# Low parts on VectorE instead of GpSimd behind attention, and weight conversions spread over w_out's products

## The chip, the cores and the metric

The kernel runs on one core of a Trainium2 chip. That core has a matrix engine (TensorE, PE in the profile, with its weight loads as PEld), three engines for elementwise work (VectorE, called DVE; ScalarE, called ACT; GpSimd, called POOL) and SyncE (SP), which here only issues DMAs. The metric is the device time of one execution in microseconds; lower is better. The kernel before took 1270.37 us, the median of three runs (1267.63 to 1270.51).

## What is computed

The reference is block-causal attention followed by a bilinear feed-forward layer, all in float32:

```python
# q, k, v: (8, 8, 576, 64), blocks of 64
scores = scale * np.matmul(q, k.transpose(0, 1, 3, 2))
scores = np.where(block_i >= block_j, scores, -1000000000.0)
attn = softmax(scores)                      # with 1e-09 in the denominator
x = (attn @ v) as (4608, 512)               # tokens x model width
a = x @ w_a ; b = x @ w_b                   # 512 -> 1536
out = (a * b) @ w_out                       # 1536 -> 512
```

The weights w_a, w_b and w_out come as float64 and are turned into float32 parts on the chip. h stands for a * b below.

## The kernel before, in words

**Number format.** TensorE multiplies in a faster float32 format of less precision. To keep precision, each operand is split into a high part (a rounding copy, made by ScalarE) and a low part (the value less its high part, a subtraction on VectorE or GpSimd). A product is then three products: high by high, high by low, low by high. `split` (L108) makes both parts: L110 is ScalarE's copy, L113 the subtraction, on the engine it is handed as `lo_eng`.

**Stages.** The hidden width of 1536 is worked in twelve blocks of 128, called f. First comes attention, head by head, and woven into it the *first pass* (`first_pass`, L545) for the blocks f = 0 to 3: for 288 tokens at a time, `ab_unit` (L228) makes a and b by 24 products each pair, multiplies them (hf, L243) and splits the result (hh by ScalarE, hl by `lo_eng[0]`, which is GpSimd, L245); `o_unit` multiplies with w_out. What of the first pass is left when the attention loop ends (L638) is emitted behind it (L784 and L796), together with the conversion of the weights for the blocks 4 to 7.

Then comes the *second pass*, for the blocks 4 to 11. It runs twice over six tiles of 768 tokens: once for the blocks 4 to 7 (tiles 0 to 5 in the text) and once for 8 to 11 (tiles 6 to 11). A tile has four units (`pair_unit`, L701), one for each f, and then w_out's products (`pair_out`, L743). A unit makes a and b for two halves of 384 tokens at once, with seven products of sums in place of eight: `sums_x` (L669) makes sums and differences of parts of x, splits them into seven high parts (L680 to L684, ScalarE) and seven low parts (L689 to L692), and that for two halves kp = 0 and 1 of the model width. A unit has 42 matmuls of 384 columns in the order y, x, w, v and then the second parts of x, w, v, each of six (twelve in a tile's first unit are taken in another order). Between them VectorE does seven operations, L729 to L739: u = x + y at L729, for which the second part of x's product waits, t = w + u at L731, for which w's waits, and so on, up to the two halves of h at L736 and L739. ScalarE makes h's high parts, GpSimd its low parts (L737 and L740). `pair_out` is 96 matmuls, run without a break in the program's order.

**Low parts of x's sums.** For kp = 0 all four instructions are on VectorE; for kp = 1 the first two (L689, L690) are on VectorE, the last two (L691, L692) on GpSimd.

**Weight conversions.** `convert_w` (L180) is a generator: each step emits a few instructions. A part of w_a and w_b (8 for four blocks) takes six steps, a part of w_out (4) five: on VectorE L139, L143, L145, L147, L149 one by one (the fifth with four small ones at L172 for the sums), ScalarE's at L140, L165 and L175, and at the end the low parts (L177, L178, or L113 for w_out). A part's raw data are fetched ahead on SyncE's queue. The parts for the blocks 8 to 11 are made during tiles 1 to 5, laid into a staging buffer `st` and stored to DRAM by SyncE's queue; they are loaded again in tile 5.

**What sets the order.** A planner at compile time orders each engine's instructions: by their place in the program and by when its model says that they can start. On the chip each engine then runs its list in order. `background(now)` (L777) fixes where in the program a conversion step stands: one step for each STEP or STEP2 ns of products counted in `k` at 2.4 columns per ns. In the second pass `k` counts the units' products (L834), not w_out's. `behind_of(ins, key)` (L117) tells the planner to put an instruction behind the last one noted under that key: conversions behind the last "hf" (L739 of the unit before), x's low parts behind "hf", and those on GpSimd behind "la" (h's last low part).

Of the kernel before, what the change touches and what calls it, by code (L numbers as in the profile page):

```python
# [14 lines left out]
ALU = mybir.AluOpType  # L15
# [23 lines left out]
MORE = 6  # L39
PREF = True  # L40
STEP = 800
STEP2 = 1900
LATE = 1
LO2 = lambda nc: nc.vector
CONVP = [1]*12
# [7 lines left out]
def attention_then_bilinear_ffn(  # L53
# [10 lines left out]
    nc = tc.nc  # L64
# [13 lines left out]
    T2 = 384  # L78
# [26 lines left out]
    def f32(ap):  # L105
        return ap.bitcast(F32)
# [10 lines left out]
    def behind_of(ins, key):  # L117
        if key in last:
            tc.add_manual_dep(ins.ins, last[key].ins.name, NOSYNC, reason="after work that is waited for")
# [35 lines left out]
    def parts(fs):  # L155
        return [(f, i) for f in fs for i in range(KP)] + [(f, KP) for f in fs]

    def new_wo(f):
        w_sb[f][1] = wopool.tile([P, 2, DO], F32R, tag="wo", name=f"wo{f}")
# [49 lines left out]
    lo_eng = [nc.gpsimd]  # L209
# [427 lines left out]
                n_moe += 1  # L637
    order.close()  # L638
    marks.clear()
    right.close()  # L640
    ps_more = ctx.enter_context(
        tc.tile_pool(name="ps_more", bufs=MORE, space=bass.MemoryType.PSUM, reuse_waits="tile"))
# [3 lines left out]
    def bank(nm):  # L646
        nonlocal n_bank
        n_bank += 1
        return (ps_mm if n_bank % 8 < 2 else ps_more).tile([P, 512], F32, tag="mm", name=nm)
# [7 lines left out]
    def new_w(f):  # L657
        w_sb[f] = [w2.tile([P, KP, 2, NW, P], F32R, tag="wab", name=f"wab{f}"), None]

    def load_x(tt):  # L660

        raw = []
        for cc in range(NCC):
            raw.append(rpool.tile([P, 2, T2], F32, tag="xr", name=f"xr{cc}_{tt}"))
            nc.sync.dma_start(
                raw[cc].rearrange("p j n -> p (j n)"), xd[cc * P:(cc + 1) * P, 2 * tt * T2:2 * (tt + 1) * T2])
        return raw

    def sums_x(raw, kp, nm):  # L669

        hi = xk.tile([P, NW, T2], F32R, tag="xh", name=f"xh_{nm}_{kp}", bufs=3)
        t = tpool.tile([P, 3, T2], F32, tag="xt", name=f"xt_{nm}_{kp}")
        a, b = raw[2 * kp:2 * kp + 2]
        v = nc.vector
        for ins in (v.tensor_tensor(t[:, 1], b[:, 1], a[:, 1], op=ALU.subtract),
                    v.tensor_tensor(a[:, 1], a[:, 1], a[:, 0], op=ALU.subtract)):
            if nm == f"0_{NT2}":
                behind_of(ins, "hf")
        v.tensor_tensor(t[:, 0], b[:, 1], a[:, 1], op=ALU.subtract)
        nc.scalar.copy(hi[:, 0:2], a)  # L680
        nc.scalar.copy(hi[:, 2:4], t[:, :2])
        v.tensor_tensor(t[:, 2], b[:, 0], t[:, 0], op=ALU.subtract)
        nc.scalar.copy(hi[:, 4:6], b)
        nc.scalar.copy(hi[:, 6], t[:, 2])  # L684
        yield
        lo = xk.tile([P, NW, T2], F32R, tag="xl", name=f"xl_{nm}_{kp}", bufs=2)
        e = nc.gpsimd if kp else v
        for k, ins in enumerate((
                v.tensor_tensor(lo[:, 0:2], a, f32(hi[:, 0:2]), op=ALU.subtract),  # L689
                v.tensor_tensor(lo[:, 2:4], t[:, :2], f32(hi[:, 2:4]), op=ALU.subtract),  # L690
                e.tensor_tensor(lo[:, 4:6], b, f32(hi[:, 4:6]), op=ALU.subtract),  # L691
                e.tensor_tensor(lo[:, 6], t[:, 2], f32(hi[:, 6]), op=ALU.subtract))):  # L692
            if nm[0] == "0" and nm != "0_0":
                behind_of(ins, "la" if k > 1 and kp else "hf")
        yield hi, lo


# [45 lines left out]
    def pair_out(fs, hs, nm, out):  # L743

        todo = [(j, o) for j in (1, 0) for o in range(NO)]
        n = {}

        def run(j, o, fs_):
            k = j, o
            if k not in n:  # L750
                n[k] = 0, bank(f"pso{j}_{o}_{nm}")[:, :T2]
            i, ps = n[k]
            osl = slice(o * P, (o + 1) * P)
            for f in fs_:
                (hh, hl), wt = hs[f][j], w_sb[f][1]
                for a, b in ((0, hh), (0, hl), (1, hh)):
                    nc.tensor.matmul(ps, wt[:, a, osl], b, start=i == 0, stop=i == 3 * len(fs) - 1)  # L757
                    i += 1
            n[k] = i, ps
            if i == 3 * len(fs):  # L760
                out(j, o, ps)

        for k in todo[:2]:
            run(*k, fs[:-1])
        for k in todo[:2]:
            run(*k, fs[-1:])
        for k in todo[2:]:
            run(*k, fs)

    for f in range(F1, F1 + F2):  # L770
        new_w(f)
# [5 lines left out]
    def background(now):  # L777
        nonlocal n_conv
        while n_conv < now:
            next(conv, None)  # L780
            n_conv += 1

    k = 0
# [8 lines left out]
    for kp in range(KP):  # L792
        g = sums_x(raw, kp, "0_0")
        next(g)
        xs.append(next(g))
# [3 lines left out]
    start, pace = k * HT / 2.4 / STEP, STEP  # L799
    k = 0  # L800


    for ps_ in range(2):
        fs = list(range(F1 + ps_ * F2, F1 + (ps_ + 1) * F2))
        for tt in range(NT2):
            lastp = ps_ == 1 and tt == NT2 - 1
            pt = {}

            def load_part(j, o):
                ts = slice((2 * tt + j) * T2, (2 * tt + j + 1) * T2)  # L810
                pt[j, o] = ppool.tile([P, T2], F32, tag="pt", name=f"pt{j}_{o}_{tt}_{ps_}"), ts
                if ps_ == 1:
                    nc.sync.dma_start(pt[j, o][0], part[o * P:(o + 1) * P, ts])

            def out(j, o, ps):
                t, ts = pt[j, o]
                if ps_ == 0:
                    nc.scalar.copy(t, ps)
                    nc.gpsimd.dma_start(part[o * P:(o + 1) * P, ts], t, accum_op=ALU.add)
                else:  # L820
                    nc.vector.tensor_tensor(t, ps, t, op=ALU.add)
                    nc.sync.dma_start(outT[o * P:(o + 1) * P, ts], t)
                i = todo.index((j, o)) + 6
                if i < len(todo):
                    load_part(*todo[i])

            todo = [(j, o) for j in (1, 0) for o in range(NO)]
            hs = {}
            nm = f"z{ps_}_{tt}"
            for i, f in enumerate(fs):  # L830
                if ps_ == 0 and tt == 0:
                    background(PER_F * (i + 1))
                for _ in pair_unit(f, xs, f"{nm}_{f}", hs, i == 0):
                    k += 1  # L834
                    background(start + k * T2 / 2.4 / pace)
                if i == 0 and not lastp:
                    raw = load_x((tt + 1) % NT2)
                if i == 1:
                    for x in todo[:6]:
                        load_part(*x)  # L840
                if i == 2 and not lastp:
                    nxt = [sums_x(raw, kp, f"{ps_}_{tt + 1}") for kp in range(KP)]
                    next(nxt[0])
                if ps_ == 0 and tt == NT2 - 1:
                    new_w(f + F2)
                    for kp in range(KP):
                        nc.sync.dma_start(
                            f32(w_sb[f + F2][0][:, kp]).rearrange("p j c n -> p (j c n)"), wabd[f - F1, kp])
            if not lastp:
                lo0 = next(nxt[0])  # L850
                next(nxt[1])
                xs = [lo0, next(nxt[1])]
            if ps_ == 0 and tt == 0:
                background(1e4)
                conv = convert_w(parts(range(F1 + F2, NF)), nc.vector, paced=True, stage=stage)
                n_conv, start, k, pace = 0, 0, 0, STEP2
            pair_out(fs, hs, nm, out)
            if ps_ == 0 and tt == NT2 - 1:
                background(1e4)
                for f in fs:  # L860
                    new_wo(f + F2)
                    nc.sync.dma_start(f32(w_sb[f + F2][1]).rearrange("p j n -> p (j n)"), wod[f - F1])
# [39 lines left out]
```

## Time and profile before

| what | value |
|---|---|
| median of three runs | 1270.37 us |
| the profiled execution | 1273.42 us, its span 1271.7 us |
| granted TensorE clock, mean | 0.994 |
| busy: PE / VectorE / ScalarE / GpSimd | 97% / 78% / 55% / 47% |
| attention's end, about | 640 us |
| w_out's products of tile 0, the part that waits last | from 733.40 us |
| a tile of the second run (1019.05 to 1065.52) | 46.47 us |

The profile shows one execution. A row of a timeline has start, length, engine, line and operation, outputs and inputs, and in brackets how long the engine stood idle before it and what ended that. A row of a group has line, engine, operation, names and shape, count, then busy time and mean ns, then the idle time before. The chain of waits is the work that ended last, followed backwards. Names: xl and xh are the low and high parts of x's sums, hl and hh (or h_z in the second pass) those of h, hf is h before the split, u_z the seven operations' results, psx_z and its like a unit's products, pso and pso_z w_out's, raww, sw, mw, xw and st the stages of a conversion, pt and part the partial output.

### The profile page before, as it was taken

Reading aid. Unit: us, or ns where it says so; the run is one execution under the profiler, and the core shown is the slowest. Engines: PE = TensorE matmul, PEld = TensorE weight load, DVE = VectorE, ACT = ScalarE, POOL = GpSimd, SP = SyncE. Lnnn points to the kernel's source line nnn. Section 1 sums busy time; section 2 is a strip of 40 time slices with the busy share of each in tenths; the row PEclk is TensorE's granted clock in tenths of the full one; section 3 lists DMA queues with packets and bytes.
Section 4 is the critical chain, followed back from the end, with each engine's and each line's share of the span. In section 5 each row is a group of like instructions: output and inputs, shape, how many; then the busy total and the mean of one; then the engine's idle time right before and its main releaser. Section 6 shows DMA issues by size and latency. Waiting matters only on the chain.

```text
span 1271.7 us, 23478 instructions
## 1 busy us (share of the span) xinstructions
PE 1238.1 (97%) x7849; PEld 1171.8 (92%) x7849; DVE 986.7 (78%) x2341; ACT 701.6 (55%) x1770; POOL 596.7 (47%) x727
## 2 busy tenths in 40 slices
PE   9998999999999999999998999999999999999998
PEld 5667998999999999999997999999999999999998
DVE  6888887877877877878789989889869577577553
ACT  4788887788788788877745434244334222122210
POOL 3667666565665665655522254254354323123231
PEclk9899999999999999999998999999999999999999
DMA  5467667767667776677224364464477542243131
GB/s 179 124 179 205 171 173 198 180 167 183 163 177 181 177 179 171 166 180 170 88 92 120 104 142 132 123 146 136 118 173 275 154 149 83 67 149 102 49 100 63
DMA packets 86585, 187.15 MB, mean 147 GB/s; under 512 B 11200, under 2 KB 46016, under 8 KB 86464
## 3 DMA queue, kind: packets, MB, share of 16 engines
q1 hardware_dynamic: 74944, 166.76, 47.0%
q0 software_dynamic: 6912, 9.44, 5.1%
q10 hardware_dynamic: 4608, 9.44, 2.0%
q8 instruction: 63, 1.03, 0.3%
q14 instruction: 58, 0.48, 0.1%
HBM read 87.03 MB, written 47.19 MB: 106 GB/s over the span
## 4 chain that ended last, share of the span: by engine, by line
PE 75%; DVE 15%; issue 3%; ACT 3%; DMA 2%; POOL 1%; SPq 0%; ACTq 0%; DVEq 0%; POOLq 0%
PE pso_z L757 16%; PE ps L217 12%; PE tp L468 7%; PE psw_z L711 6%; PE psx_z L711 6%; PE psv_z L711 5%; PE pso L217 5%; PE s L392 4%; PE av L517 3%; PE av L523 3%; PE psy_z L711 3%; PE sl L392 2%; DVE sw L147 2%; DVE nm L398 1%; DMA kp<-kT 1%
## 5 line engine op out<-in xcount | busy, mean ns | idle before, releaser
L113 POOL TENSOR_TENSOR h_z<-u_z,h_z 128x384 fp32r<-128x384 f32 x96 | 110.2, 1149 | 331.7 <-ACT h_z L110 315.1
L217 PE MATMUL ps<-xh,wab 128*128 128x288 f32 x1024 | 241.6, 303 | 1.2 <-ACT a L241 1.2
L445 POOL TENSOR_SCALAR e<-e,rc 128x512 f32<-128x512 f32 (+3 forms) x256 | 151.1, 602 | 130.5 <-DVE rc L442 122.6
L757 PE MATMUL pso_z<-h_z,wo 128*128 128x384 f32 x1152 | 203.0, 335 | 0.7 <-POOL h_z L113 0.7
L757 PEld LDWEIGHTS pso_z<-h_z,wo 128*128 128x128 f32 x1152 | 199.8, 188 | 1.9 <-POOL h_z L113 1.9
L217 PEld LDWEIGHTS ps<-xh,wab 128*128 128x128 f32 x1024 | 171.9, 188 | 4.7 <-ACT a L241 1.4
L472 DVE TENSOR_TENSOR al<-tp,ah 128x512 fp32r<-128x512 f32 x224 | 131.5, 608 | 30.3 <-ACT ah L470 29.8
L217 PE MATMUL ps<-xl,wab 128*128 128x288 f32 x512 | 154.0, 301 | 0.0
L470 ACT CAST ah<-tp 128x512 fp32r<-128x512 f32 x224 | 116.5, 532 | 51.6 <-PE tp L468 48.8
L468 PE MATMUL tp<-ident,e 128*128 128x128 f32 x832 | 134.7, 276 | 8.2 <-POOL e L445 3.0
L110 ACT CAST h_z<-u_z 128x384 fp32r<-128x384 f32 x96 | 49.3, 514 | 161.5 <-DVE u_z L736 157.4
L217 PE MATMUL pso<-hh,wo 128*128 128x288 f32 x512 | 128.4, 312 | 4.4 <-ACT hh L110 4.4
L711 PE MATMUL psx_z<-xh,wab 128*128 128x384 f32 x384 | 117.8, 342 | 5.6 <-DVE u_z L729 5.2
L401 ACT ACTIVATE e<-s,nm 128x192 f32<-128x192 f32 (+2 forms) x192 | 101.4, 528 | 36.1 <-DVE nm L398 26.9
L468 PEld LDWEIGHTS tp<-ident,e 128*128 128x128 f32 x832 | 100.0, 140 | 22.4 <-issue 9.5
L711 PE MATMUL psw_z<-xh,wab 128*128 128x384 f32 x384 | 116.9, 340 | 0.5 <-DVE u_z L731 0.4
L711 PE MATMUL psv_z<-xh,wab 128*128 128x384 f32 x384 | 116.5, 338 | 0.1
L398 DVE TENSOR_REDUCE nm<-s 128x1 f32<-128x192 f32 (+3 forms) x256 | 109.9, 431 | 2.4
L217 PEld LDWEIGHTS ps<-xl,wab 128*128 128x128 f32 x512 | 96.4, 188 | 3.4
L217 PEld LDWEIGHTS pso<-hh,wo 128*128 128x128 f32 x512 | 88.7, 192 | 6.6 <-ACT hh L110 5.3
L113 POOL TENSOR_TENSOR v<-vr,v 128x320 fp32r<-128x320 f32 x56 | 50.2, 896 | 87.5 <-ACT v L110 72.7
L392 PE MATMUL s<-k,q 128*128 128x256 f32 x336 | 81.0, 321 | 2.5 <-ACT e_s L401 2.1
(144 smaller groups left out, 2970.4 us busy)
## 6 DMA issues: line engine op xcount, KB each, us to landing
k<-kp SPq DMA_DIRECT2D x112, 288.0 KB, 3.7
xr<-xd SPq DMA_DIRECT2D x48, 384.0 KB, 3.5
q<-qp SPq DMA_DIRECT2D x112, 160.0 KB, 2.6
raww<-wab SPq DMA_DIRECT2D x24, 512.0 KB, 3.7
qp<-qT SPq DMA_DIRECT2D x32, 320.0 KB, 3.2
vr<-vm SPq DMA_DIRECT2D x64, 160.0 KB, 2.9
kp<-kT SPq DMA_DIRECT2D x32, 288.0 KB, 3.3
xd<-xf ACTq DMA_DIRECT2D x32, 288.0 KB, 3.1
```

The costliest lines, as they stand in the source:

```text
L110: nc.scalar.copy(hi, src)
L113: return lo_eng.tensor_tensor(lo, src, f32(hi), op=ALU.subtract)
L217: mm = nc.tensor.matmul(ps, w_, d_, start=(i == 0), stop=(i == n - 1))
L392: mark = nc.tensor.matmul(ps[:, :w], qm[:, q0[t]:q0[t] + P], kk[:, :w], start=(i == 0), stop=(i == len(ks) - 1))
L398: nc.vector.tensor_reduce(nm[:, t:t + 1], view, axis=AX.X, op=ALU.max, negate=True)
L401: nc.scalar.activation(out, view, AF.Exp, bias=bias, accum_out=sm[:, t, :1])
L445: nc.gpsimd.tensor_scalar(ev, ev, rc[:, t:t + 1], 1.0, op0=ALU.mult, op1=ALU.mult)
L468: mark = nc.tensor.transpose(tp[:, c], src, ident)
L470: nc.scalar.copy(ah[:, :m, cols], tp[:, :m])
L472: return nc.vector.tensor_tensor(al[:, :m, cols], tp[:, :m], f32(ah[:, :m, cols]), op=ALU.subtract)
L711: nc.tensor.matmul(ps, wt[:, i, iw], j[:, ix], start=start and kp == 0 and i == 0 and j is xh, stop=kp == KP - 1 and i == 1, skip_group_ch ...
L757: nc.tensor.matmul(ps, wt[:, a, osl], b, start=i == 0, stop=i == 3 * len(fs) - 1)
```

## The change

Three edits. The low parts of h of the first pass that are emitted behind the attention loop go to VectorE. All low parts of x's sums go to VectorE, all ordered behind "hf". And `pair_out` becomes a generator: after each of w_out's products the caller counts it in `k` and may emit conversion steps, while the pace STEP2 goes from 1900 to 3200 ns for a step.

```diff
-STEP2 = 1900
+STEP2 = 3200
...
     order.close()
     marks.clear()
+    lo_eng[0] = nc.vector
...
         lo = xk.tile([P, NW, T2], F32R, tag="xl", name=f"xl_{nm}_{kp}", bufs=2)
-        e = nc.gpsimd if kp else v
-        for k, ins in enumerate((
+        for ins in (
                 v.tensor_tensor(lo[:, 0:2], a, f32(hi[:, 0:2]), op=ALU.subtract),
                 v.tensor_tensor(lo[:, 2:4], t[:, :2], f32(hi[:, 2:4]), op=ALU.subtract),
-                e.tensor_tensor(lo[:, 4:6], b, f32(hi[:, 4:6]), op=ALU.subtract),
-                e.tensor_tensor(lo[:, 6], t[:, 2], f32(hi[:, 6]), op=ALU.subtract))):
+                v.tensor_tensor(lo[:, 4:6], b, f32(hi[:, 4:6]), op=ALU.subtract),
+                v.tensor_tensor(lo[:, 6], t[:, 2], f32(hi[:, 6]), op=ALU.subtract)):
             if nm[0] == "0" and nm != "0_0":
-                behind_of(ins, "la" if k > 1 and kp else "hf")
+                behind_of(ins, "hf")
...
                 for a, b in ((0, hh), (0, hl), (1, hh)):
                     nc.tensor.matmul(ps, wt[:, a, osl], b, start=i == 0, stop=i == 3 * len(fs) - 1)
                     i += 1
+                    yield
...
         for k in todo[:2]:
-            run(*k, fs[:-1])
+            yield from run(*k, fs[:-1])
         for k in todo[:2]:
-            run(*k, fs[-1:])
+            yield from run(*k, fs[-1:])
         for k in todo[2:]:
-            run(*k, fs)
+            yield from run(*k, fs)
...
-            pair_out(fs, hs, nm, out)
+            for _ in pair_out(fs, hs, nm, out):
+                k += 1
+                background(start + k * T2 / 2.4 / pace)
```

## The prediction

> **What bounds the kernel now.** I read the page's busy shares first, then the table of stretches from the end of attention on, then the chain of waits, and last single instructions in order of time.
>
> ```profile
> PE 1238.1 (97%) x7849; PEld 1171.8 (92%) x7849; DVE 986.7 (78%) x2341; ACT 701.6 (55%) x1770; POOL 596.7 (47%) x727
> ```
>
> TensorE (PE) is nearly always busy, so only its holes can be won. The change touches nothing ahead of attention's end, so the holes that count lie from about 640 us on, in two places.
>
> ```profile
> 640.00:660.00 20.00, 19.11 (x143) 18.66 (x142) 19.80 (x39) 7.75 (x19) 5.27 (x5) 1.00 0.30 99
> 660.00:680.00 20.00, 17.65 (x131) 17.21 (x131) 19.38 (x43) 9.33 (x22) 4.10 (x4) 1.00 0.34 109
> 680.00:700.00 20.00, 16.11 (x96) 15.09 (x94) 19.52 (x33) 12.46 (x25) 7.10 (x5) 0.83 0.47 138
> 700.00:716.50 16.50, 16.50 (x94) 16.26 (x94) 16.50 (x32) 7.76 (x13) 2.37 (x3) 1.00 0.46 156
> 716.50:733.40 16.90, 16.16 (x89) 15.05 (x88) 16.55 (x31) 8.38 (x15) 6.24 (x6) 1.00 0.09 31
> ```
>
> **Place A, 640 to 733 us** (columns: stretch, length, PE, weight load, VectorE, ScalarE, GpSimd, granted clock, DMA share, GB/s): the rest of the first pass and the units of the second pass's first tile, under the conversion of the next weights. VectorE is busy 91.75 of 93.40 us, 98%; PE stands for 7.87 us, and from 680 to 700 us its clock is 0.83. So here VectorE sets the pace.
>
> ```profile
> 747.02 0.53 PE psy_z L711 x3
> ...
> 972.73 16.64 PE pso_z L757 x96
> ...
> 1019.05 16.79 PE pso_z L757 x96
> ...
> 1065.52 16.78 PE pso_z L757 x96
> ```
>
> **Place B, tiles 1 to 5 of the second pass** (chain of waits: start, length, what). Tile 0's products end about 747.02, tile 5's at 972.73 + 16.64 = 989.37: five tiles in 242.35 us, 48.47 each. From 1019.05 to 1065.52, where nothing is converted any more, a tile takes 46.47. So the five lose 242.35 - 5 x 46.47 = 10.0 us, 0.67 for each of their fifteen units after a tile's first (in a tile's first unit VectorE has time left). How such a loss arises, in the tile from 844 us:
>
> ```profile
> 861.75 0.96 DVE L139 TENSOR_SCALAR sw<-raww 128x512 int32<-128x512 int32 x1
> 862.62 1.24 DVE L143 TENSOR_SCALAR mw<-raww 128x512 int32<-128x512 int32 x1
> 863.79 0.55 DVE L729 TENSOR_TENSOR u_z<-psx_z,u_z 128x384 f32<-128x384 f32 x1
> ```
>
> ```profile
> 861.39 2.19 POOL L113 TENSOR_TENSOR h_z<-u_z,h_z 128x384 fp32r<-128x384 f32 x2 [6.42 <-ACT h_z L110]
> ```
>
> ```profile
> 864.39 0.44 PE L711 MATMUL psx_z<-xh,wab 128*128 128x384 f32 x1 [0.64 <-DVE u_z L729]
> ```
>
> Two conversion instructions stand ahead of the sum at L729 while GpSimd makes two low parts of h; PE then stands 0.64 us for L729, and a little more in restarting. The tiles from 1019 us on have the same sums and the same GpSimd work without conversions, and lose nothing.
>
> **The change, part by part.** *Low parts from GpSimd to VectorE.* The rows of place A, first GpSimd's work as it is, then the nearest VectorE rows of the same shapes:
>
> ```profile
> L113 POOL TENSOR_TENSOR hl<-hf,hh 128x288 fp32r<-128x288 f32 x10 | 10.4, 1039 | 43.2 <-ACT hh L110 43.2
> ```
>
> ```profile
> L243 DVE TENSOR_TENSOR hf<-ps,a 128x288 f32<-128x288 f32 x10 | 4.5, 449 | 0.0
> ...
> L691 DVE TENSOR_TENSOR xl<-xr,xh 128x768 fp32r<-128x768 f32 x1 | 0.9, 946 | 0.0
> ```
>
> Ten low parts of h move (the units emitted behind the attention loop), and two low parts of x's sums. Added to VectorE: 10 x 0.449 + 0.946 + 0.55 (L729's, of 384 columns too) = 6.0 us at most; as its instructions overlap at their ends (below, 691.00 + 0.95 reaches past the next start, 691.87), about 5. Against it stands what GpSimd's instructions do to VectorE's today:
>
> ```profile
> 685.64 0.42 DVE L139 TENSOR_SCALAR sw<-raww 128x512 int32<-128x512 int32 x1
> ...
> 690.80 0.28 DVE L172 TENSOR_TENSOR mw<-mw,xw 128x128 f32<-128x128 f32 x1
> 691.00 0.95 DVE L689 TENSOR_TENSOR xl<-xr,xh 128x768 fp32r<-128x768 f32 x1
> 691.87 0.88 DVE L172 TENSOR_TENSOR mw<-xw,mw 128x128 f32<-128x128 f32 x1
> ...
> 696.82 2.61 DVE L690 TENSOR_TENSOR xl<-xt,xh 128x768 fp32r<-128x768 f32 x1
> 699.36 1.24 DVE L139 TENSOR_SCALAR sw<-raww 128x512 int32<-128x512 int32 x1
> ```
>
> ```profile
> 691.13 1.47 POOL L113 TENSOR_TENSOR hl<-hf,hh 128x288 fp32r<-128x288 f32 x1 [2.75 <-ACT hh L110]
> ...
> 696.10 2.52 POOL L691 TENSOR_TENSOR xl<-xr,xh 128x768 fp32r<-128x768 f32 x1 [3.49 <-ACT xh L683]
> 698.58 1.74 POOL L692 TENSOR_TENSOR xl<-xt,xh 128x384 fp32r<-128x384 f32 x1
> ```
>
> L172 takes 0.28 us, and 0.88 beside GpSimd's low part of h: 0.60 lost. The 128x768 subtraction takes 0.95, and 2.61 beside GpSimd's L691; L139 takes 0.42, and 1.24 beside L692: 1.66 + 0.82 lost. I take 0.60 for each of the ten, as the one shown has: 6.0 + 2.5 = 8.5 us of VectorE's time come back for the 5 to 6 added. **Net gain 2.5 to 3.5 us; I take 3.0.** As VectorE sets the pace, it is place A that gets shorter. Two unknowns bound it. The new instruction waits for ScalarE's high part, and everything behind it in VectorE's line waits too:
>
> ```profile
> PE pso L217 <- ACT hh L110: 4.4, 4, 1.6
> PEld pso L217 <- POOL hl L113: 3.7, 4, 1.1
> ...
> PE pso_z L757 <- POOL h_z L113: 0.7, 1, 0.7
> DVE wab L178 <- ACT wab L175: 0.7, 2, 0.3
> ```
>
> The nearest such wait is L178's for ScalarE, in the last row: two waits of 0.35 us on average. Behind the held instruction stand conversions and the next product of a and b, for whose h PE waits (4.4 us in the first row). Were each of the ten held like that, 3.5 us, place A would lose 0.5 in place of gaining 3.0. The other way round, the clock of 0.83 costs 16.11 x 0.17 = 2.7 us; if it stays up because PE stands less, the gain is 3.5 + 2.7 = 6.2. Both ends stay in the range; I keep 3.0, since only two instructions of L178's kind were held at all.
>
> In the later tiles the same two low parts (six on VectorE instead of four) lie between the last unit and the next tile: 4 x 0.95 + 2 x 0.95 + 2 x 0.55, at most 6.8 us in the 16.64 us of w_out's products. Nothing waits for them before the next tile's first products, so I cost them at nothing; without that cover they would cost 1.5 us a tile. In the tiles without conversions PE has no hole to give: gain nothing.
>
> *The conversions' pace.* The twelve conversions have 8 x 6 + 4 x 5 = 68 steps. Today a step falls due per 1.9 us of the units' products at 0.16 us (384 columns by the code's 2.4 per ns), one per 11.9 products, and w_out's products don't count. Between a unit's start and L729's place in the program lie 24 products: 2.0 steps. After it a step falls due per 20 products, w_out's counted: 24 / 20 = 1.2 steps in that place, and about five during w_out's products, where PE needs VectorE for nothing in this pass. Place for them: 16.64 us, less 6.8 for x's low parts, for five steps of up to 1.24 us, the longest conversion shown above, 6.2: it fits, with x's low parts ahead of them in the program. If it didn't, the next tile would start late.
>
> Counting from tile 0's w_out products on (96 of them, then 264 a tile), I place every 20th. Of the fifteen units, three get two steps ahead of L729 (two in tile 1, one in tile 5), one in tile 3 gets the long step (L149 with four L172), and eleven get one short step. One short step ends before L729 is due: six products take 0.53 x 2 = 1.06 us, L729 can start after twelve (2.12) and must be done after twenty-four (4.24), which leaves about 1.5 us beside its own 0.55; a locked conversion costs 0.96 to 1.24. So eleven units should lose nothing, and four keep 0.67 (the mean) to 0.9: 2.7 to 3.6 us, I take 3.1. **Gain 10.0 - 3.1 = 6.9 us.** Bounds: 0, if the planner of the order again packs two ahead of L729, and 10.0.
>
> The moved steps also issue DMAs on SyncE's queue: the fetch of the next weights and the store of the converted ones, the same number, now also between w_out's products and so ahead of loads of x and of w_out's weights. x is summed a tile ahead (three high buffers), that is the cover. The last step falls due at product 68 x 20 = 1360, that is 40 products into tile 5's w_out products (today still in its units); its w_out weights are first read about 1019.05, thirty us later. Cost nothing; if that cover were gone, PE would wait there once.
>
> **Sum.** 3.0 + 6.9 = 9.9 us off the profiled execution's 1273.42 (span 1271.7) gives 1263.5. That execution lies 3.05 us over the median of the three runs, 1270.37; taken off, **1260.5 us**.
>
> **One rule weighed.** VectorE is 98% busy in place A, and the change hands it work of a 47% busy engine. The Trainium skill, "Perfetto Trace Analysis", section "Optimizing Scalar/DVE Operations", says that with VectorE saturated it may make sense to give work away, to GpSimd too, though the two share a read port and it might not help. Its first half speaks against the change: by it place A grows by 6.0 us; its second half is what the rows at 691 and 696 us show, and by them it shrinks by 3.0.
>
> **Rivals.**
> 1. *The saturated engine.* VectorE's time for the ten and the two is added (6.0 us), and what GpSimd gave up doesn't come back, since other instructions run into the low parts of h that stay on GpSimd. For it: the 98%. Against it: of the 8.5 us each piece stands beside one of the moved instructions. Time: 1260.5 + 3.0 + 6.0 = 1269.5.
> 2. *The pace does nothing.* The holes come from GpSimd's low parts of h, which stay; the planner, which orders VectorE, pulls w_out's steps away and still puts two ahead of L729. For it: 861.39 to 863.58 is h's, not x's. Against: a step is held behind the unit before it, so it can't move up. Time: 1260.5 + 6.9 = 1267.4.
> 3. *All holes close*, and the clock stays up: 10.0 + 6.2 = 16.2 in place of 9.9: 1254.2.
> 4. *Slower: h's last low part late.* Six low parts of x now run on VectorE right beside GpSimd's last two of h, and w_out's products wait for these (0.7 us already at 733 us, third of the four wait rows). If each of the two is blocked by one more 0.95 us subtraction, a tile loses 1.9: over the eleven other tiles 20.9, 1281.4. It decides from 9.9 / 11 = 0.9 us a tile. Against it: the first four of the six are there today, and tiles of 46.47 have no room for such a wait.
>
> **How the numbers follow.** Forecast 0.58 (its own range 1257 to 1264), rival 1 0.09, rival 2 0.14, rival 3 0.14, rival 4 0.05. A measurement of this kernel tells 0.3%, 3.8 us, from no change: faster is below 1266.6. Forecast and rival 3 lie there, 0.72; of rival 2, with some of the gain left, 0.06, of rival 1 0.02: 0.80. Slower is rival 4, 0.05; the rest, 0.15, is no change. The range takes in rival 3's 1254.2 and goes to 1268, just past rival 2; rival 1's upper part, rival 4 and the tail below are left out.
>
> **What would show it.** In the changed kernel's trace: place A's end (tile 0's w_out products, 733.40 now) 3 us earlier; conversions of 0.28 and 0.42 there no longer 0.88 and 1.24 before tile 0; tiles 1 to 5 at about 47.1 instead of 48.5, and one conversion instruction ahead of L729 instead of two; conversions among w_out's products; tiles from 1019 us on still 46.47. The prediction is wrong if VectorE shows idle time ahead of the low parts of h (then place A gains nothing), if units still have two conversions ahead of L729, or if w_out's products wait for GpSimd's h.

## The result, and the profile after

The changed kernel takes 1261.9 us (median of six runs, 1256.25 to 1263.39), the kernel before, run beside it and earlier, 1271.0 (six runs, 1267.63 to 1274.2). The ratio is 0.9923, with a 95% interval of 0.99 to 0.9945: faster by 0.8%. The forecast was 1260.5 beside 1270.37, a ratio of 0.992.

The page's first row after the change; GpSimd lost 60 us of busy time, VectorE 20, though VectorE has the work that GpSimd gave up:

```profile
PE 1226.2 (98%) x7849; PEld 1167.9 (93%) x7849; DVE 966.3 (77%) x2375; ACT 700.2 (56%) x1770; POOL 536.9 (43%) x693
```

The two profiled executions differ by 17.2 us of span, more than the medians. 7.75 us of that lie ahead of the change's first instruction: attention's last product at L523 starts at 638.71 us before and at 630.95 after, with the same work up to there. So everything below is read from stretches with the same work in every kernel: from that product to tile 0's first product (psy_z), from there to tile 0's last w_out product, and on to tile 5's last. The table of stretches (stretch, length, then busy time of PE, weight load, VectorE, ScalarE, GpSimd, then clock, DMA share, GB/s), the kernel before:

```profile
638.71:698.96 60.25, 53.12 (x368) 51.17 (x367) 58.34 (x115) 29.73 (x64) 15.42 (x14) 0.94 0.36 110
698.96:746.69 47.73, 46.99 (x266) 45.64 (x265) 45.72 (x77) 21.83 (x39) 19.84 (x16) 1.00 0.42 122
746.69:989.04 242.35, 236.09 (x1322) 229.00 (x1321) 203.93 (x319) 92.95 (x174) 101.84 (x91) 1.00 0.58 156
```

and the changed kernel:

```profile
630.95:684.52 53.57, 51.46 (x367) 50.28 (x366) 52.28 (x123) 29.54 (x64) 2.17 (x2) 0.97 0.35 115
684.52:734.23 49.71, 47.48 (x265) 45.31 (x264) 46.37 (x79) 20.71 (x37) 14.01 (x14) 1.00 0.46 125
734.23:971.88 237.65, 233.88 (x1322) 230.37 (x1321) 194.68 (x330) 92.52 (x173) 81.36 (x81) 1.00 0.57 158
```

Place A, the first two rows, goes from 107.98 to 103.28 us: 4.7 won. Place B, the third row, goes from 242.35 to 237.65: 4.7 won. Together 9.4, where 9.9 were forecast as 3.0 + 6.9. The six tiles behind take 278.65 in both.

**Place A.** VectorE is busy 58.34 + 45.72 = 104.06 us before and 52.28 + 46.37 = 98.65 after, 5.4 less; but these rows don't hold the same work, for in the changed kernel some sums of x fall behind their end. From the same start to the end of tile 0's last L739 VectorE's work differs by the twelve moved instructions alone (188 rows for 176). There it is busy 2.5 us less, and the stretch is 2.8 us shorter; the kernel before, then the changed one:

```profile
638.71:731.62 92.91, 85.78 (x549) 82.80 (x548) 90.64 (x176) 44.77 (x91) 23.30 (x20) 0.96 0.34 108
630.95:721.06 90.11, 86.25 (x559) 83.18 (x557) 88.13 (x188) 45.06 (x91) 9.01 (x9) 0.98 0.35 111
```

VectorE's instructions in order of time after the change (start, length, engine, line):

```profile
675.86 0.46 DVE L113 TENSOR_TENSOR hl<-hf,hh 128x288 fp32r<-128x288 f32 x1
...
681.05 0.29 DVE L172 TENSOR_TENSOR mw<-mw,xw 128x128 f32<-128x128 f32 x1
...
685.60 0.95 DVE L690 TENSOR_TENSOR xl<-xt,xh 128x768 fp32r<-128x768 f32 x1
686.47 0.95 DVE L691 TENSOR_TENSOR xl<-xr,xh 128x768 fp32r<-128x768 f32 x1
```

The low part of h costs 0.46 us and is not held; L172's 0.88 and L690's 2.61 of before are gone. What still runs beside GpSimd's low parts of h of the second pass (720.75 to 723.46 here) is still slow:

```profile
720.98 1.60 DVE L689 TENSOR_TENSOR xl<-xr,xh 128x768 fp32r<-128x768 f32 x1
722.50 1.77 DVE L690 TENSOR_TENSOR xl<-xt,xh 128x768 fp32r<-128x768 f32 x1
```

The waits in place A:

```profile
PE pso L217 <- DVE hl L113: 1.1, 2, 0.8
PE pso L217 <- ACT hh L110: 0.8, 1, 0.8
DVE wab L178 <- ACT wab L175: 0.3, 1, 0.3
```

PE's wait for h's high part has gone from 4.4 us to 0.8. In the first stretch PE stands 2.11 us (53.57 - 51.46) where it stood 7.13 (60.25 - 53.12). The other 1.7 of the 6.7 us won there are PE's busy time (51.46 for 53.12), and go with its clock, 0.97 for 0.94. That clock is at half speed for about 6.8 us before and 3.4 us after; in the run e1_moves below, with the same instructions up to tile 0, it stays at 1.00. A piece of each (the kernel before, the changed one, e1_moves):

```profile
690.40:696.80 6.40, 5.23 (x20) 4.89 (x21) 6.40 (x12) 6.07 (x12) 2.17 (x2) 0.50 0.59 156
679.00:682.20 3.20, 3.20 (x15) 3.20 (x14) 3.20 (x9) 3.20 (x6) 0.00 (x0) 0.50 0.62 183
682.10:685.30 3.20, 3.20 (x26) 3.20 (x26) 3.20 (x9) 3.20 (x6) 0.00 (x0) 1.00 0.70 185
```

What brings the clock down stays open: the changed kernel and e1_moves stand equally long up to tile 0 (2.11 us each). Tile 0 itself takes 2.0 us longer than before, 49.71 for 47.73.

**Place B.** The five tiles took 48.51, 48.75, 48.68, 48.63 and 47.79 us before (from last w_out product to last w_out product), and take 48.95, 46.69, 47.00, 46.97 and 48.03 now. Tile 1 got longer. VectorE's line in the window of tile 0's w_out products and the start of tile 1:

```profile
728.14 0.55 DVE L692 TENSOR_TENSOR xl<-xt,xh 128x384 fp32r<-128x384 f32 x1
728.61 0.41 DVE L139 TENSOR_SCALAR sw<-raww 128x512 int32<-128x512 int32 x1
728.94 0.41 DVE L143 TENSOR_SCALAR mw<-raww 128x512 int32<-128x512 int32 x1
731.41 0.56 DVE L676 TENSOR_TENSOR xt<-xr,xr 128x384 f32<-128x384 f32 x1 [2.05 <-DMA xr<-xd]
731.88 0.69 DVE L145 SCALAR_TENSOR_TENSOR mw<-raww,mw 128x512 f32<-128x512 uint16 x1
733.17 0.69 DVE L147 SCALAR_TENSOR_TENSOR sw<-raww,sw 128x512 int32<-128x512 int32 x1 [0.60 <-ACT sw L140]
...
739.78 0.56 DVE L683 TENSOR_TENSOR xt<-xr,xt 128x384 f32<-128x384 f32 x1
740.25 0.55 DVE L729 TENSOR_TENSOR u_z<-psx_z,u_z 128x384 f32<-128x384 f32 x1
```

```profile
740.86 0.45 PE L711 MATMUL psx_z<-xh,wab 128*128 128x384 f32 x1 [2.05 <-DVE u_z L729]
```

After x's last low part and two conversion instructions VectorE is held 2.05 us by the next load of x, with ten more conversion instructions and eight sums of x in line behind; L729 comes last, and PE stands for it, in a tile's first unit, where before it never stood.

### The profile page after: what moved, and what is told of

It is laid out like the page before. It is cut to its first block, busy times and chain, and to the rows that moved or that the text cites. A ratio compares the mean times of both kernels' runs of the same rounds, so it can differ in the third digit from the quotient of the medians.

```text
span 1254.5 us, 23460 instructions
## 1 busy us (share of the span) xinstructions
PE 1226.2 (98%) x7849; PEld 1167.9 (93%) x7849; DVE 966.3 (77%) x2375; ACT 700.2 (56%) x1770; POOL 536.9 (43%) x693
## 3 DMA queue, kind: packets, MB, share of 16 engines
HBM read 87.03 MB, written 47.19 MB: 107 GB/s over the span
## 4 chain that ended last, share of the span: by engine, by line
PE 79%; DVE 14%; ACT 2%; issue 2%; DMA 2%; POOL 1%; SPq 0%; ACTq 0%; DVEq 0%; POOLq 0%
PE pso_z L757 15%; PE ps L217 13%; PE psx_z L711 7%; PE tp L468 7%; PE psw_z L711 7%; PE psv_z L711 6%; PE pso L217 6%; PE s L392 4%; PE psy_z L711 3%; PE av L523 3%; PE av L517 3%; PE sl L392 2%; DVE sw L147 1%; DVE nm L398 1%; DVE mw L145 1%
```

## The experiments

Lengths in us, worked out as above from each kernel's trace. "To tile 0" is the first stretch, and "place A" the sum of the first two; the ratio is against the kernel before on the same chip. One thing besides the edits moves the first column: seven runs have the changed kernel's instructions up to tile 0, and there e4_late and e7_hdve take 53.6 us like it, with a clock of 0.97, while the five others (e1_moves, e5_x00, e8_hdve_x00, e9_hdve_late, e10_half) take 52.0 with 1.00. Tile 0 gives half of that back, so 0.8 us of place A between such runs is the clock and no edit.

| kernel | to tile 0 | tile 0 | place A | tiles 1 to 5 | ratio (95% interval) |
|---|---|---|---|---|---|
| before | 60.25 | 47.73 | 107.98 | 242.35 | 1 |
| changed | 53.57 | 49.71 | 103.28 | 237.65 | 0.9923 (0.99 to 0.9945) |
| e1_moves | 52.04 | 50.43 | 102.47 | 243.49 | 0.9962 (0.9946 to 0.9978) |
| e2_pace | 60.30 | 47.75 | 108.05 | 235.59 | 0.995 (0.9929 to 0.9971) |
| e3_hl | 53.57 | 54.26 | 107.83 | 242.73 | 0.9998 (0.9983 to 1.0013) |
| e6_xl | 60.04 | 48.40 | 108.44 | 243.21 | 1.0005 (0.9992 to 1.0018) |
| e4_late | 53.58 | 49.70 | 103.27 | 236.36 | 0.9894 (0.9872 to 0.9916) |
| e5_x00 | 52.02 | 50.52 | 102.54 | 237.01 | 0.9918 (0.9901 to 0.9935) |
| e7_hdve | 53.57 | 49.71 | 103.28 | 235.78 | 0.9913 (0.9894 to 0.9932) |
| e8_hdve_x00 | 52.01 | 50.54 | 102.55 | 232.84 | 0.9896 (0.9872 to 0.992) |
| e9_hdve_late | 52.02 | 50.54 | 102.56 | 233.86 | 0.9898 (0.9875 to 0.9921) |
| e10_half | 52.01 | 50.53 | 102.54 | 233.56 | 0.9907 (0.9888 to 0.9926) |

### The moves alone

```diff
-STEP2 = 3200
+STEP2 = 1900
...
             for _ in pair_out(fs, hs, nm, out):
-                k += 1
-                background(start + k * T2 / 2.4 / pace)
+                pass
```

> The change without its third edit: the low parts go to VectorE, the pace stays at 1900 ns and w_out's products emit no conversion steps. Place A is read from attention's last products (L523) to tile 0's last w_out product: 107.98 us before, 103.28 after, so 4.7 won; the five tiles behind it 242.35 before, 237.65 after, 4.7 won. Theory (two edits, two places): place A 103.3, tiles 1 to 5 within 1 us of 242.4, total about 4.7 us under the kernel before. Rival (VectorE's time in a tile is one account): x's low parts without GpSimd beside them free some 3 us of VectorE per tile, the conversions move up into it, and the tiles gain 2 us or more by this edit alone.

Measured 0.9962. The stretches:

```profile
634.10:686.14 52.04, 49.93 (x367) 48.74 (x366) 50.74 (x121) 28.30 (x62) 2.16 (x2) 1.00 0.36 114
686.14:736.57 50.43, 47.26 (x265) 45.14 (x264) 47.01 (x81) 21.66 (x41) 14.70 (x14) 1.00 0.46 127
736.57:980.06 243.49, 236.23 (x1322) 228.75 (x1321) 201.25 (x335) 94.36 (x175) 82.02 (x82) 1.00 0.58 157
```

Place A wins 5.5 us, of which 0.8 is the clock; the tiles win nothing (243.49, a little over the 1 us that the theory allowed), and tile 1 takes 49.47 in place of 48.51. The rival falls: what x's low parts free per tile is not spent on conversions where PE waits for them. VectorE is 2.7 us less busy over the five tiles and PE gains nothing.

### The pace alone

The changed kernel with `lo_eng[0] = nc.vector` taken out and x's last two low parts of kp = 1 back on GpSimd.

> The change's third edit alone: conversion steps also between w_out's products, one per 3200 ns; all low parts stay where they were, on GpSimd. Theory (two places): place A 107 to 109 us as before, tiles 1 to 5 at 237 to 239, total about 4.7 us under the kernel before. Rival (the edits need each other): x's low parts on VectorE and GpSimd hold each other up in w_out's window, the steps that are now due there don't fit, and the tiles win at most 2.5 us, with PE waiting at the first unit of several tiles and not of tile 1 alone.

Measured 0.995. Place A stays (108.05); the third stretch:

```profile
742.01:977.60 235.59, 233.19 (x1322) 230.00 (x1321) 197.86 (x312) 88.79 (x168) 101.81 (x90) 1.00 0.58 159
```

The five tiles take 46.70, 46.70, 47.07, 47.05 and 48.06: 6.8 us won, more than the theory's 237 to 239 allowed, and no wait of tile 1's first unit. The rival falls, in the other direction even: the pace is worth more without the moves than with them. The two parts alone add up to 5.5 + 6.8 = 12.3 us; the change, with both, won 9.4. Of the 2.9 us between, 0.8 is place A's clock and 2.1 is place B (237.65 for 235.59).

### h's low parts alone

```diff
     order.close()
     marks.clear()
+    lo_eng[0] = nc.vector
```

> The kernel before with one line more: h's low parts of the first pass behind attention on VectorE; x's low parts and the pace as before. Theory (the ten instructions block ten of VectorE's by 0.6 us each and cost 0.37): place A wins 2 to 3 us of the 4.7, the rest belongs to x's two low parts. Rival (what counts is PE's wait for the low part, 1.1 us long on GpSimd and 0.45 on VectorE): place A wins 4 us or more by this line alone, and PE's waits for h's low part fall from 2.7 us to about 1.

Measured no difference, 0.9998. Both expectations miss: tile 0 begins as early as in the changed kernel (53.57 for 60.25), and tile 0 gives it all back.

```profile
635.91:689.48 53.57, 51.46 (x368) 50.28 (x366) 52.27 (x123) 29.57 (x64) 4.10 (x3) 0.97 0.36 115
689.48:743.74 54.26, 48.30 (x266) 47.08 (x264) 45.40 (x77) 22.09 (x39) 24.40 (x18) 0.97 0.39 110
```

GpSimd's two low parts of x, which it still makes, in order of time, and VectorE beside them (its line numbers are one higher here):

```profile
687.54 6.38 POOL L692 TENSOR_TENSOR xl<-xr,xh 128x768 fp32r<-128x768 f32 x1 [46.57 <-ACT xh L684]
693.88 1.01 POOL L693 TENSOR_TENSOR xl<-xt,xh 128x384 fp32r<-128x384 f32 x1
```

```profile
690.57 0.95 DVE L691 TENSOR_TENSOR xl<-xt,xh 128x768 fp32r<-128x768 f32 x1
691.44 0.42 DVE L139 TENSOR_SCALAR sw<-raww 128x512 int32<-128x512 int32 x1
691.77 0.42 DVE L143 TENSOR_SCALAR mw<-raww 128x512 int32<-128x512 int32 x1
697.81 0.56 DVE L676 TENSOR_TENSOR xt<-xr,xr 128x384 f32<-128x384 f32 x1 [5.62 <-DMA xr<-xd]
```

The subtraction that took 2.52 us before takes 6.38: VectorE works without a gap, at full speed, until 692.19, and GpSimd's instruction ends 1.73 us after that. Here the one that is held up is GpSimd. The buffers of x that it reads come free late, the next load of x comes late, VectorE is held for it 5.62 us, and PE stands 4.19 us for the sum at L730 behind that. In this tile 0 the clock is 0.97, for 1.00 before, which is worth some 1.6 us more (54.26 x 0.03).

### x's low parts alone

The kernel before with the change's second edit, the four instructions `v.tensor_tensor` all behind "hf".

> The kernel before with the second edit alone: all low parts of x's sums on VectorE; h's low parts on GpSimd, pace as before. h's move alone won nothing (place A 107.83): tile 0 began 6.7 us earlier, but GpSimd's low part of x (L692 there) took 6.38 us beside VectorE's and tile 0 gave all of it back. Theory A (the two moves need each other): place A 106 to 108, at most 2 us won. Theory B (x's low parts alone carry the gain): place A 103 to 104. By both, tile 1 at 49 to 49.5 as with both moves, if x's low parts on VectorE are what delays the load of x there.

Measured no difference, 1.0005. Theory A holds in the main, the moves need each other, though place A's 108.44 lies just outside its 106 to 108: up to tile 0 nothing changes (60.04 for 60.25), since PE there waits for h, not for x. Tile 1 takes 49.26 for 48.51, nearly as in the run with both moves: that loss belongs to x's low parts.

### The second conversions start later

```diff
-STEP2 = 3200
+STEP2 = 3000
...
             for _ in pair_out(fs, hs, nm, out):
-                k += 1
-                background(start + k * T2 / 2.4 / pace)
+                if ps_ or tt:
+                    k += 1
+                    background(start + k * T2 / 2.4 / pace)
```

> The whole change, but the second conversions start behind tile 0's w_out products (none of their steps there), at 3000 ns a step. In the changed kernel tile 1 loses 2.3 us at its first unit, and takes 48.95 us. Theory (tile 0's w_out window is overfilled: six low parts of x, ten conversion instructions and the sums of x in line, with VectorE held for a load of x in between): that wait is gone, tile 1 takes 46.5 to 47.5, tiles 2 to 5 are as in the changed kernel within 0.5 each, about 1.5 to 2.5 us under the changed kernel. Rival (the wait at tile 1's first unit comes from the load of x, not from the conversions): tile 1 still takes 48 or more.

Tile 1 takes 47.09 in place of 48.95. Three conversion instructions still stand in VectorE's line between x's low parts and L729, for twelve in the changed kernel; with these few the wait is nearly gone, though VectorE is held for the loads of x longer than in the changed kernel (2.26 and 1.73 us, for 2.05). But tile 2 now takes 47.94, with a wait at its first unit; the five tiles win 1.3 us over the changed kernel, less than expected.

### x's low parts on VectorE in place A only

```diff
-        for ins in (
+        e = nc.gpsimd if kp and nm != "0_0" else v
+        for k, ins in enumerate((
...
-                v.tensor_tensor(lo[:, 4:6], b, f32(hi[:, 4:6]), op=ALU.subtract),
-                v.tensor_tensor(lo[:, 6], t[:, 2], f32(hi[:, 6]), op=ALU.subtract)):
+                e.tensor_tensor(lo[:, 4:6], b, f32(hi[:, 4:6]), op=ALU.subtract),
+                e.tensor_tensor(lo[:, 6], t[:, 2], f32(hi[:, 6]), op=ALU.subtract))):
             if nm[0] == "0" and nm != "0_0":
-                behind_of(ins, "hf")
+                behind_of(ins, "la" if k > 1 and kp else "hf")
```

> The whole change, except that x's low parts go to VectorE only for the first sums (tile 0's); from tile 1's on the last two of kp = 1 stay on GpSimd as in the kernel before. Stages so far: place A 103.3 us and tiles 1 to 5 237.65 in the changed kernel; 108.05 and 235.59 with the pace alone. Theory (x's low parts on VectorE win in place A only, and in tile 1 they hold up the loads of x and cost the 2.2 us at its first unit): place A 103 to 104, tiles 1 to 5 235.6 +- 0.7, tile 1 at 46.7, about 2 us under the changed kernel. Rival (tile 1's wait comes from place A's end being earlier, whoever makes x's low parts): tile 1 still 48.5 or more, no gain.

Tile 1 takes 47.25, although tile 0 begins even earlier than in the changed kernel (52.02 for 53.57, by the clock): the rival falls. VectorE's line in tile 0's window has all twelve conversion instructions, but no hold for x. The five tiles take 237.01, not the 235.6 expected within 0.7, for tile 4 now takes 47.98 (46.97 in the changed kernel), with a wait of its first unit. Why the planner's order puts it there was not followed up.

### h's low parts on VectorE in tiles 1 to 5 too

```diff
+        lo_h = nc.vector if nm[:2] == "z0" and nm[:4] != "z0_0" else nc.gpsimd
...
-        split(hb, lb, t, nc.scalar, nc.gpsimd)
+        split(hb, lb, t, nc.scalar, lo_h)
...
-        last["la"] = split(ha, la, u, nc.scalar, nc.gpsimd)
+        last["la"] = split(ha, la, u, nc.scalar, lo_h)
```

> The whole change, and h's low parts too on VectorE in tiles 1 to 5 of the second pass (eight 128x384 subtractions a tile more for VectorE, none left on GpSimd there). Theory (what is left of the holes in tiles 1 to 5 comes from conversions of 0.96 to 1.5 us beside GpSimd's low parts of h): conversions take 0.42 to 0.69 throughout, the holes at units two to four nearly close, tiles 2 to 4 at 46.5 to 46.7, tiles 1 to 5 together 234 to 236. Rival (VectorE's time is the limit, not the port): the 3.7 us more per tile make the holes larger, tiles 1 to 5 at 239 or more, and w_out's products wait for h's low parts.

Tiles 2, 3 and 5 take 46.32, 46.32 and 46.37: the holes of units two to four are closed. The cause shows in VectorE's groups over the five tiles (count, busy time, mean ns). The changed kernel:

```profile
L147 DVE SCALAR_TENSOR_TENSOR sw<-raww,sw 128x512 int32<-128x512 int32 x11 | 10.9, 991 | 1.0 <-ACT sw L140 1.0
...
L143 DVE TENSOR_SCALAR mw<-raww 128x512 int32<-128x512 int32 x11 | 7.1, 649 | 0.0
```

and this one:

```profile
L147 DVE SCALAR_TENSOR_TENSOR sw<-raww,sw 128x512 int32<-128x512 int32 x11 | 7.5, 684 | 0.6 <-ACT sw L140 0.6
...
L143 DVE TENSOR_SCALAR mw<-raww 128x512 int32<-128x512 int32 x11 | 4.6, 420 | 0.0
```

So the same instructions take 684 and 420 ns where GpSimd has no subtractions, for 991 and 649 (what GpSimd still does in these tiles is add partial outputs to DRAM by DMA, part<-pt). VectorE has forty subtractions more and is busy 189.26 us in the stretch, less than the 194.68 of the changed kernel. Tiles 1 and 4 still take 48.81 and 47.96, again by one wait each at the first unit, so the expectation for tile 4 (46.5 to 46.7) misses; ahead of tile 4's stands this hold:

```profile
878.10 0.56 DVE L676 TENSOR_TENSOR xt<-xr,xr 128x384 f32<-128x384 f32 x1 [2.70 <-DMA xr<-xd]
```

### Three combinations

The run above, first with x's low parts as in e5_x00, second with the late start of e4_late, third with w_out's products counted half (`k += 0.5`) at 2560 ns a step.

> The changed kernel with h's low parts of tiles 1 to 5 on VectorE and, from tile 1 on, the last two of x's low parts of kp = 1 on GpSimd. With h's move alone tiles 2, 3 and 5 took 46.32 to 46.37 and tiles 1 and 4 still 48.81 and 47.96, by one wait at the tile's first unit each. Theory (those first waits come from VectorE's line in w_out's window, which is too full with x's six low parts, conversions, and a hold for the next load of x): with two of them on GpSimd the line is 1.3 us shorter and x's buffers come free sooner; tile 1 at 47 or less, the five tiles at 233 to 235, place A 102.5 to 103.3. Rival (a hold for the load alone decides, and it falls where the planner puts the sum): the first waits stay or move to other tiles, the five at 235.5 or more.

> The changed kernel with h's low parts of tiles 1 to 5 on VectorE and no conversion steps in tile 0's w_out products (3000 ns a step). The late start alone took tile 1 from 48.95 to 47.09 but had 47.94 in tile 2. Theory (first-unit waits come from conversions beside a hold for x in the window): tile 1 at 46.4 to 47.1, one other tile may keep 1 to 2 us; the five at 233 to 235. Rival (VectorE's time over the tile is too full with h's low parts): several tiles above 47, the five at 236 or more.

> The changed kernel with h's low parts of tiles 1 to 5 on VectorE, w_out's products counted half and 2560 ns a step: 3 steps in w_out's window instead of 4.8, 10.5 in the units instead of 8.4. Theory (the window is overfilled, and without GpSimd beside them conversions in the units are cheap, 0.42 to 0.69 us): first-unit waits of tiles 1 and 4 shrink to under 1 us, units stay without holes; the five at 232.5 to 234.5. Rival (units are the tight place even without GpSimd): holes return at units two to four, the five at 236 or more.

The first gives the shortest stretch of all:

```profile
735.29:968.13 232.84, 231.97 (x1322) 230.90 (x1321) 192.29 (x358) 93.37 (x174) 53.15 (x51) 1.00 0.59 163
```

Its tiles take 46.90, 46.32, 46.32, 46.11 and 47.19, and no first unit loses more than 0.6 us. Tile 5's 0.9 us over the others is w_out's products waiting for a low part of h, which VectorE makes now. The second keeps one long wait, of tile 2 (48.47), behind another kind of hold: the last steps of a conversion wait for ScalarE, which writes the staging buffer.

```profile
790.51 0.56 DVE L177 TENSOR_TENSOR st<-xw,st 128x384 fp32r<-128x384 f32 x1 [3.11 <-ACT st L165]
```

The third keeps tile 1's wait as it was (48.48), with 2.37 us of hold for x; that part of its expectation fails, the rest (units without holes, and tile 4) holds. Its edit did not thin the window, though: VectorE's line there has eleven conversion instructions ahead of L729, for twelve in the changed kernel (that the planner brings steps of tile 1's first unit forward would explain it, but was not followed up). So it doesn't tell what fewer would do. Going by place B, the first is 4.8 us ahead of the changed kernel (232.84 for 237.65); the 0.7 us in place A goes with the clock. Its ratio, 0.9896, is lower than the changed kernel's 0.9923 too, but the intervals overlap, the two ran on different chips, and e4_late has 0.9894 with a longer place B; it was faster than the kernel before beyond doubt, and than the changed one by the stretches only.

## Why the prediction was right, and where it was not

**The total** was right: 9.9 us forecast, 9.4 by the stretches, 9.1 by the medians. That it came so close is luck: place A gave 1.7 us more than forecast and place B 2.2 less, each for reasons that the forecast did not have.

**Place A: 3.0 forecast, 4.7 measured.** The prices were right, and so was the account of VectorE's time. The twelve moved instructions added what was said (a low part of h 0.46 us, for 0.449), the 0.88 and 2.61 beside them went, and up to tile 0's last L739 VectorE came out 2.5 us less busy and 2.8 us earlier, where 3.0 was said. The bound below nothing, a hold of each for ScalarE, did not come: the only hold for it in the waits is L178's 0.3. The other 1.9 us lie behind that L739, and the forecast had no term for them. Of w_out's 96 products 24 run ahead of the point at which PE waits for GpSimd, for 19 before; and that point comes 0.76 us behind L739 (721.82), for 1.78 (733.40), as GpSimd's low part of h there takes 1.02 us for 1.72. The clock, which the forecast priced at 2.7 us and kept for the upper end, was at one half for 6.8 us before and 3.4 after in these two executions, some 3.4 and 1.7 us of full speed.

What was wrong is to add up the two moves as separate savings, 6.0 us for the ten and 2.5 for the two. Alone, each won nothing. Up to tile 0 it is h's low parts that count, since PE waits for them, and they win 6.7 us (60.25 to 53.57, alone or with x's). Within tile 0 VectorE has no room for so early a start: with x's low parts left on GpSimd all of it is given back (54.26), with them on VectorE 2.0 us (49.71). In e3_hl VectorE is less busy than in the changed kernel up to tile 0's last unit, 85.2 us for 88.1, and gains nothing by it, for it is held.

**Place B: 6.9 forecast, 4.7 measured.** The pace by itself won 6.8, as forecast. What failed is the pair of sentences on w_out's window: that x's two low parts there cost nothing, and that five steps "fit" after them. The window was filled up with lengths alone, 6.8 + 6.2 of 16.64 us. Two of x's eight low parts were longer than said (7.7 us in all, beside GpSimd's of h). It left out the eight sums of the next x, which the planner also puts there, and above all that an engine in line is held: with the last low parts of x at the end of VectorE's line, x's buffers come free later and the next load holds VectorE for 2.05 us in tile 0's window. L729 then comes 3 us late, and PE loses 2.3 us in a unit that the forecast had left out of its fifteen. That it takes both, the hold for x and the conversions, is shown by three groups of runs. Tile 1's first unit loses 0 to 0.6 us with twelve conversion instructions in that line and no hold for x (e2_pace, e5_x00, e8_hdve_x00), 0.2 to 0.9 with holds and three or four (e1_moves, e4_late, e9_hdve_late), and 2.2 to 2.5 with both (the changed kernel, e7_hdve, e10_half).

**The fifteen units** kept about 3.4 us of loss, where 3.1 was forecast, but the count behind that was wrong. It put two conversions, or the long step, ahead of L729 in four units and one in eleven. The trace has two or more in thirteen and one in two: a step falls due per 20 products, 2.1 in a unit's 42, and most of them stand between L739 and the next L729, not only those due in the 24 products ahead of it. This is a sign of being wrong that the prediction had named itself. Seven units lost 0.2 to 0.4 us, and one in tile 5, where three sums of x stand among them, 1.3; the others lost next to nothing. One such pair after the change:

```profile
760.80 1.01 DVE L139 TENSOR_SCALAR sw<-raww 128x512 int32<-128x512 int32 x1
761.73 1.24 DVE L143 TENSOR_SCALAR mw<-raww 128x512 int32<-128x512 int32 x1
762.89 0.55 DVE L729 TENSOR_TENSOR u_z<-psx_z,u_z 128x384 f32<-128x384 f32 x1
```

It is as slow as the pair from 861.75 us before, but it starts 1.4 us behind its unit's first product (759.44), for 2.2 (859.53): before, L177 and L178 of an earlier step stood in line ahead of L735 there and made it late. So the nearness of 3.4 to 3.1 is luck as well. The floor was a little off too. A tile without any hole takes 46.32 us (e7_hdve); the 46.47 taken from the second run holds 0.15 of that run's own, whose w_out products take 16.79 us for 16.64. So the kernel before lost 10.7 us in the five tiles, not 10.0. That these holes come from GpSimd's low parts of h beside VectorE, and not from VectorE's load, is shown by e7_hdve.

**The rivals.** The saturated engine (1) fell: VectorE's time shrank. The Trainium skill, "Perfetto Trace Analysis", section "Optimizing Scalar/DVE Operations", was borne out in its second half alone: with VectorE at 98%, work taken back from GpSimd made VectorE less busy, 90.64 to 88.13 us up to tile 0's last unit. The idle pace (2) had its premise, two conversions still ahead of L729, but not its outcome: e2_pace won 6.8 us. That all holes close (3) was not reached by the change, but nearly by e8_hdve_x00 in place B (232.84 us, for five tiles of 46.47 or 232.35). The slower case (4) fell: w_out's products wait for GpSimd's h 0.5 us in all.

## What to carry to other kernels

Where VectorE and GpSimd work at the same time, look up how long the same instruction takes with and without the other beside it, before judging which of them has room: taking work away from the idle one can make the busy one less busy. Price a window that several things move into by its holds too, not by the lengths alone: in an engine's line, one wait for a load stands ahead of everything behind it. And when edits touch the same engine, run each alone: here two halves won nothing singly and some 5 us together, and another pair lost 2 of the sum of its parts. Compare the granted clock of two stretches before their lengths: here the same instructions took 53.57 us and 52.04.

## What was not expected of the hardware

GpSimd can be held far longer than one VectorE instruction: its subtraction of 128x768 took 6.38 us (2.52 beside one long VectorE instruction in the kernel before), while VectorE ran a row of instructions at full speed and GpSimd's ended 1.73 us behind the last. The Trainium skill, "SBUF — State Buffer", section "Who interferes with whom", has the two engines share a port pair that the one issued first keeps for the whole instruction, the other being blocked. The kernel before agrees: VectorE's subtraction from 696.82 us ended at 699.43, 0.81 us behind the end of GpSimd's at 698.62. In e3_hl it went otherwise: GpSimd's instruction starts at 687.54, and seven of VectorE's, which start at 687.76 and later, are done ahead of it.

Work that no edit touches moved the totals: up to attention's last product the profiled executions took from 630.95 us (the changed kernel) to 638.71 (the kernel before) and 639.92 (e10_half), and the first row of transposes started anywhere from 15.7 to 22.7 us. The difference of two spans, 17.2 us, would have been read as nearly twice the effect.
